# Tail queries and tail x of two batches: transposed by the DMA instead of TensorE

## Chip, cores and metric

The kernel runs on one core of a Trainium2 chip. The metric is the device time in microseconds, the median of several runs. A core has TensorE (PE, matrix multiplication; PEld is its loading of weights), VectorE (DVE), ScalarE (ACT), GpSimd (POOL) and SyncE (SP). SP and POOL issue DMA transfers here; PE writes only to PSUM, so what it transposes has to be copied to SBUF by DVE or ACT.

## The reference

A linear attention with cosine weights, followed by a two-layer network. In short:

```python
batch, n_heads, seq, head_dim = (8, 8, 576, 64)      # q, k, v
phi(x) = concat(relu(x) * cos_w, relu(x) * sin_w)    # 64 -> 128 features
kv  = einsum('bhsf,bhsd->bhfd', phi(k), v);  z = sum over s of phi(k)
num = einsum('bhsf,bhfd->bhsd', phi(q), kv)
den = einsum('bhsf,bhf->bhs', phi(q), z) + 1e-06
x   = (num / den), as [4608 tokens, 512]
out = relu(x @ w_in)**2 @ w_out                      # w_in 512 x 2048, w_out 2048 x 512
```

## The kernel before

A batch has 576 positions. 512 of them are four pieces of 128 (J = 4, pieces j = 0 to 3); the other 64 are the tail (j = 4). The tail's eight heads are laid out as two halves of 64 partitions, so a tail tile has 128 partitions and half the columns. Two batches share one tail tile of the network's input, xTt, so the tails of batches 0 and 1 are multiplied together.

Attention of one piece goes in steps. `att_feat` makes the features of the queries (qp, for the tail qpt): DVE the cosine half (L171), ACT the sine half (L181). The features are then transposed, either by PE (`att_qT_pe`, L284, into the PSUM tile tq) with a copy to qpTp (`att_qT_copy`, L293), or by a DMA on SP's queue (`att_qT`, L267, straight into qpT). `att_d` multiplies them by kvz (num, L310, on PE) and divides (den, rden and x on DVE, L320 to L324; the tail of x is xt). x is transposed in turn, by PE with a copy (`att_x_pe`, L351 and L356, into the PSUM tile tx) or by a DMA on SP's queue (`att_x`, L342), into xT or, for the tail, xTt.

The network runs after it: `gemm1` multiplies xT by the weights w1sb (hps, L383, on PE), ACT applies the relu (rt, L391), DVE squares (gT, L398); `gemm2` and `pair_mm` multiply by w2sb and by sums of its blocks (L432, L456, L525).

The order of work is written out by hand. The network's work is cut into slots, each some 2 us of PE; `gemm1` of batch 0 is slots 0 to 7, `gemm2` of batch 0 is 8 to 15, `gemm1` of batch 1 is 16 to 25 with the tails in the last two, 24 and 25. Pieces of attention of later batches are hung behind a slot with `at(slot, function, ...)`, and `run` issues slot by slot. `plan` does this for all pieces of a batch, from lists of slots: k, f (features of the queries), kv, d (division), and, where the lists t and x are given, the slots of the transposes on PE. Where t and x are empty, the transposes go by DMA. Only batch 1 gives t and x; batch 0's pieces are placed by hand. Each engine takes its own instructions in this order and waits by semaphores for the others; a DMA on SP's queue starts as soon as its sources are written and SP has issued what stands before it.

POOL's queue loads the weights and batches 1 to 3; SP's queue loads batch 0 at the start and batches 4 to 7 later, and carries all DMA transposes.

Of the kernel before, what the change touches and what calls it, by code (L numbers as in the profile page):

```python
# [19 lines left out]
def kernel(  # L20
# [18 lines left out]
    J = S // P  # L39
# [586 lines left out]
    def at(s, fn, *args):  # L626
        after.setdefault(s, []).append((fn, args))
# [9 lines left out]
    def plan(b, k, f, kv, d, t=(), x=(), act_cos=(1, 3), act_v=range(NS)):  # L637


        for j in range(NS):  # L640
            last = j == J or j % 2
            at(k[j], att_k, b, j, feat_cos_act if j in act_cos else feat_cos)
            at(k[j], att_v, b, j, nc.scalar if j in act_v else nc.vector)
            at(f[j], att_feat, b, j)
            if t:
                at(t[j], att_t, b, j)
            elif last:
                at(f[j], att_qT, b, j // 2)
            at(d[j], att_d, b, j)
            if x:  # L650
                at(x[j], att_x_pe, b, j, x[j] > 16)
            elif last:
                at(d[j], att_x, b, j // 2)
        for i in range(2):
            at(kv[i], att_kv, b, i)


    for j in (2, 3):
# [4 lines left out]
    at(2, att_d, 0, 3)  # L663
    at(3, att_x_pe, 0, 3, True, nc.vector.tensor_copy)
    at(12, att_feat, 0, J)
    at(17, att_t, 0, J)
    at(18, att_d, 0, J)
    at(19, att_x_pe, 0, J, True)
    plan(
        1,  # L670
        k=(8, 8, 8, 9, 9),
        f=(4, 5, 6, 12, 13),
        kv=(10, 10),
        d=(11, 13, 15, 17, 19),
        t=(5, 6, 7, 16, 17),
        x=(12, 14, 16, 18, 20),
        act_cos=(),
        act_v=(),
    )
    at(14, load_batch, 3, nc.gpsimd, "qkv")  # L680
    plan(
        2,
        k=(21, 22, 23, 24, 25),
        f=(18, 19, 20, 22, 23),
# [3 lines left out]
        act_v=(1, 3),  # L688
    )
    plan(  # L690
        3,
        k=(29, 31, 32, 34, 35),
        f=(27, 30, 33, 34, 34),
# [4 lines left out]
    for b in range(4, B):  # L698
# [6 lines left out]
            f=(o + 4, o + 4, o + 5, o + 5, o + 6),  # L705
# [99 lines left out]
```

## Time and profile before

| what | before |
|---|---|
| median of 8 runs | 290.05 us (289.21 to 291.23) |
| the profiled execution | 290.23 us, span 288.4 us |
| PE busy | 281.8 us (98%), 3045 matmuls |
| DVE, ACT busy | 202.3 us (70%), 163.6 us (57%) |
| PE's granted clock | 1.00 throughout |
| DMA | 53.04 MB, mean 184 GB/s |

The page is read from the profiled execution. Busy times of an engine are sums of its instructions without overlap; a row of the timeline gives the start in us from the span's start, the duration, the engine, the line, the operation with the tile written and the tile read, and the count where equal instructions are merged. PE's matmuls are pipelined, so a row's duration reaches into the next row.

### The profile page before, as it was taken

What the parts mean: (1) busy time and instruction counts of PE and PEld (TensorE: products, weight loads), DVE (VectorE), ACT (ScalarE), POOL (GpSimd) and SP (SyncE); (2) the same over time, 40 slices, a digit from 0 to 9 for tenths busy, and PEclk for the clock granted to TensorE, in tenths of its full rate; (3) what the DMA queues carried; (4) which work ended last, traced back from release to release, by engine and by line L of the source; (5) the groups of instructions that cost most, each with busy time, mean ns of one, the idle gap of its engine ahead of it and who ended that gap; (6) DMA issues with size and microseconds to landing.
All of it is one profiled execution on the core that took longest, in us unless ns stands there. A gap on an engine that the chain in (4) does not pass through costs nothing.

```text
span 288.4 us, 7293 instructions
## 1 busy us (share of the span) xinstructions
PE 281.8 (98%) x3045; PEld 235.5 (82%) x3045; DVE 202.3 (70%) x452; ACT 163.6 (57%) x249; POOL 38.9 (14%) x67
## 2 busy tenths in 40 slices
PE   8999999999999999999999999999999999999995
PEld 3569845789678888898988888888998988889884
DVE  1367674687499399887597776977677877547485
ACT  3476753579759759455782358835695551155210
POOL 1462503860000000100002000000000000000002
PEclk9999999999999999999999999999999999999999
DMA  7999995999737998899519995399828540300015
GB/s 215 287 205 282 350 209 188 319 370 315 130 107 190 161 327 187 197 287 239 167 76 204 331 189 164 93 251 300 175 70 209 140 49 2 125 23 0 2 73 148
DMA packets 76785, 53.04 MB, mean 184 GB/s; under 512 B 52016, under 2 KB 71984, under 8 KB 76752
## 3 DMA queue, kind: packets, MB, share of 16 engines
q1 hardware_dynamic: 66960, 29.24, 44.4%
q0 software_dynamic: 9648, 23.20, 27.2%
q8 instruction: 24, 0.39, 0.5%
q10 hardware_dynamic: 144, 0.13, 0.1%
q14 instruction: 9, 0.07, 0.1%
HBM read 36.70 MB, written 9.44 MB: 160 GB/s over the span
## 4 chain that ended last, share of the span: by engine, by line
PE 80%; DMA 8%; issue 2%; ACT 2%; POOL 2%; DVE 2%; SPq 2%; ACTq 0%; POOLq 0%
PE hps L383 38%; PE ya L525 9%; PE yc L525 9%; PE yu L525 7%; PE yv L525 5%; PE num L310 3%; DMA q<-in_q_dram 3%; DMA qt<-in_q_dram 3%; PE kz L241 3%; DMA out_dram<-ysb 3%; PE yps L456 2%; SPq L69 1%; PE tq L284 1%; DVE ysb L537 1%; PE yps L432 1%
## 5 line engine op out<-in xcount | busy, mean ns | idle before, releaser
L383 PEld LDWEIGHTS <-w1sb 128*128 128x128 bf16 x1312 | 112.6, 98 | 13.0 <-issue 2.0
L383 PE MATMUL hps<-xT,w1sb 128*128 128x256 bf16 (+1 forms) x1056 | 119.1, 269 | 0.7 <-ACT rt L391 0.2
L391 ACT ACTIVATE rt<-hps 128x1024 bf16<-128x1024 f32 x72 | 73.6, 1022 | 66.1 <-PE hps L383 43.7
L398 DVE TENSOR_TENSOR gT<-rt 128x1024 bf16<-128x1024 bf16 x64 | 44.0, 687 | 21.1 <-ACT rt L391 21.0
L525 PEld LDWEIGHTS <-gs 128*128 128x128 bf16 x480 | 46.7, 98 | 5.6
L525 PEld LDWEIGHTS <-gT 128*128 128x128 bf16 x312 | 29.7, 98 | 3.5
L410 POOL DMA_DIRECT2D out_dram<-ysb x14 | 7.6, 544 | 171.0 <-DVE ysb L537 145.0
L181 ACT ACTIVATE kp<-k,sin_col 128x512 bf16<-128x512 f32 x32 | 22.4, 717 | 3.3 <-DMA k<-in_k_dram 3.3
L324 DVE TENSOR_TENSOR x<-num,rden 128x512 bf16<-128x512 f32 x32 | 22.1, 692 | 1.1
L181 ACT ACTIVATE qp<-q,sin_col 128x512 bf16<-128x512 f32 x32 | 22.1, 721 | 0.7 <-DMA q<-in_q_dram 0.7
L320 DVE TENSOR_SCALAR den<-num 128x8 f32<-128x8 f32 (+1 forms) x40 | 6.5, 164 | 20.8 <-PE num L310 20.6
L521 DVE TENSOR_TENSOR gs<-gT 128x1024 bf16<-128x1024 bf16 x26 | 17.8, 684 | 0.0
L171 DVE TENSOR_SCALAR qp<-q,cos_col 128x512 bf16<-128x512 f32 x32 | 15.2, 501 | 1.7 <-DMA q<-in_q_dram 1.7
L525 PE MATMUL ya<-w2t,gs 128*128 128x256 bf16 x120 | 15.6, 273 | 0.0
L525 PE MATMUL yc<-w2sb,gs 128*128 128x256 bf16 x120 | 15.6, 273 | 0.0
L525 PE MATMUL yu<-w2t,gs 128*128 128x256 bf16 x120 | 15.5, 273 | 0.0
L383 PE MATMUL hps<-xTt,w1sb 128*128 128x128 bf16 x256 | 15.1, 219 | 0.2 <-ACT rt L391 0.2
L200 ACT CAST vext<-v 128x512 bf16<-128x512 f32 x23 | 14.1, 614 | 1.7 <-DMA v<-in_v_dram 1.7
L525 PE MATMUL yu<-w2sb,gs 128*128 128x256 bf16 x112 | 14.5, 273 | 0.0
L576 ACT COPY s<-yu 128x256 f32<-128x256 f32 x14 | 5.2, 372 | 15.6 <-PE yu L525 15.6
L525 PE MATMUL yc<-w2sb,gT 128*128 128x256 bf16 x104 | 13.5, 273 | 0.0
L525 PE MATMUL yv<-w2t,gT 128*128 128x256 bf16 x104 | 13.5, 273 | 0.0
(97 smaller groups left out, 334.8 us busy)
## 6 DMA issues: line engine op xcount, KB each, us to landing
out_dram<-ysb POOLq DMA_DIRECT2D x14, 512.0 KB, 3.9
k<-in_k_dram SPq DMA_DIRECT2D x5, 1024.0 KB, 8.3
v<-in_v_dram SPq DMA_DIRECT2D x5, 1024.0 KB, 9.4
q<-in_q_dram SPq DMA_DIRECT2D x5, 1024.0 KB, 5.6
q<-in_q_dram POOLq DMA_DIRECT2D x3, 1024.0 KB, 12.6
k<-in_k_dram POOLq DMA_DIRECT2D x3, 1024.0 KB, 9.1
v<-in_v_dram POOLq DMA_DIRECT2D x3, 1024.0 KB, 8.8
w1sb<-in_moe_w_in_dram POOLq DMA_DIRECT2D x4, 512.0 KB, 9.2
```

Of the source, the lines that this page charges most:

```text
L171: nc.vector.tensor_scalar(out=dst[:, :, 0:D], in0=src, scalar1=0.0, scalar2=cos_col[:, j : j + 1], op0=ALU.max, op1=ALU.mult,)
L181: nc.scalar.activation(out=dst[:, :, D:F], in_=src, func=ACTF.Relu, scale=sin_col[:, j : j + 1])
L200: copy(out=vx[:, j, h0:h1, 0:D], in_=piece("v", b, j)[:, h0:h1, :])
L241: nc.tensor.matmul(out=kz[:, half, hh * E1 : (hh + 1) * E1], lhsT=lhsT, rhs=rhs, start=(j == 0 and hh == 0), stop=(j == J and hh == HH - 1),)
L310: nc.tensor.matmul(out=out, lhsT=lhsT, rhs=kvz[:, half * HH + hh, :], start=True, stop=True)
L324: nc.vector.tensor_tensor(out=x_of(b, j).rearrange("p (b k) (l d) -> p b k l d", b=n, l=2), in0=n4[:, :, :, 0:D].rearrange("p b (k l) d -> ...
L383: nc.tensor.matmul(out=out, lhsT=w1sb[:, kb, hb * P : (hb + 1) * P], rhs=rhs, start=(kb == 0), stop=(kb == KB - 1),)
L391: nc.scalar.activation(out=rt[:, :, :], in_=hps[:, :, :], func=ACTF.Relu)
L398: nc.vector.tensor_tensor(out=dst, in0=rt[:, :, :], in1=rt[:, :, :], op=ALU.mult)
L410: eng.dma_start(out=dst, in_=y.rearrange("p i c -> p (i c)") if n > 1 else y[:, c0:c1])
L521: nc.vector.tensor_tensor(out=t[:, :, :], in0=in0, in1=in1, op=op)
L525: nc.tensor.matmul(out=acc, lhsT=lhs[:, hb, :], rhs=rhs[:, hb, :], start=(hb == 0), stop=(hb == HB2 - 1),)
```

## The change

The tail (j = 4) of batches 0 and 1 leaves PE. Its query features are transposed by `att_qT`, and its x by `att_x`, both DMAs on SP's queue. In `plan` the test for the lists t and x becomes one for each piece, and batch 1's lists lose their last entry. The pieces 0 to 3 of these batches stay on PE, and the other batches have been on the DMA for all pieces.

```diff
@@ plan
-            if t:
+            if j < len(t):
                 at(t[j], att_t, b, j)
             elif last:
-                at(f[j], att_qT, b, j // 2)
+                at(max(f[j], 15), att_qT, b, j // 2)
             at(d[j], att_d, b, j)
-            if x:
+            if j < len(x):
                 at(x[j], att_x_pe, b, j, x[j] > 16)
             elif last:
                 at(d[j], att_x, b, j // 2)
@@ batch 0
     at(12, att_feat, 0, J)
-    at(17, att_t, 0, J)
+    at(15, att_qT, 0, J // 2)
     at(18, att_d, 0, J)
-    at(19, att_x_pe, 0, J, True)
+    at(18, att_x, 0, J // 2)
@@ batch 1
         d=(11, 13, 15, 17, 19),
-        t=(5, 6, 7, 16, 17),
-        x=(12, 14, 16, 18, 20),
+        t=(5, 6, 7, 16),
+        x=(12, 14, 16, 18),
```

In the instruction order PE loses eight transposes of qpt (L284) and four of xt (L351), each a weight load and a matmul. DVE loses two copies of tq, ACT two copies of tx. SP gains four DMA transposes, ahead of the first one of batch 2.

## Prediction

> **What bounds the kernel now.** I read the page first, for the engine that has no slack.
>
> ```profile
> PE 281.8 (98%) x3045; PEld 235.5 (82%) x3045; DVE 202.3 (70%) x452; ACT 163.6 (57%) x249; POOL 38.9 (14%) x67
> ...
> PE 80%; DMA 8%; issue 2%; ACT 2%; POOL 2%; DVE 2%; SPq 2%; ACTq 0%; POOLq 0%
> ```
>
> TensorE (PE) is busy 281.8 of 288.4 us and is 80% of the chain that ended last. A matmul taken off PE is worth its place in PE's row, unless what replaces it arrives later than PE wants it. So I read PE's timeline where the twelve transposes stand (start, duration, line, tile).
>
> ```profile
> 56.07 1.91 PE L383 MATMUL hps<-xT,w1sb 128*128 128x256 bf16 x16
> 57.81 0.39 PE L284 MATMUL tq<-ident,qpt 128*128 128x128 bf16 x4
> 58.04 0.41 PE L310 MATMUL num<-kvz,qpTp 128*128 128x65 bf16 x8
> 58.28 0.39 PE L284 MATMUL tq<-ident,qpt 128*128 128x128 bf16 x4
> 58.51 1.91 PE L383 MATMUL hps<-xT,w1sb 128*128 128x256 bf16 x16
> 60.34 0.32 PE L310 MATMUL num<-kvz,qpTp 128*64 128x65 bf16 x8
> 60.59 0.40 PE L351 MATMUL tx<-ident,x 128*128 128x128 bf16 x4
> 60.83 1.91 PE L383 MATMUL hps<-xT,w1sb 128*128 128x256 bf16 x16
> 62.58 0.28 PE L351 MATMUL tx<-ident,xt 128*128 128x128 bf16 x2
> 62.78 0.32 PE L310 MATMUL num<-kvz,qpTp 128*64 128x65 bf16 x8
> 63.03 1.92 PE L383 MATMUL hps<-xT,w1sb 128*128 128x256 bf16 x16
> 64.79 0.28 PE L351 MATMUL tx<-ident,xt 128*128 128x128 bf16 x2
> 64.90 5.40 PE L383 MATMUL hps<-xT,w1sb 128*128 128x256 bf16 x48
> 70.14 1.95 PE L383 MATMUL hps<-xTt,w1sb 128*128 128x128 bf16 x32
> ```
>
> The rows overlap: a duration holds the pipeline's depth, and the next row starts before it ends. The distance from start to start is what PE pays. The three groups of 16 from 64.90 to 70.14 take 5.24 us, 1.75 each, and no idle time stands in these rows. The last line is the first reader of the tails, xTt. PE's timeline a little further on, and ScalarE's (ACT's), show the one wait nearby:
>
> ```profile
> 72.32 1.95 PE L383 MATMUL hps<-xTt,w1sb 128*128 128x128 bf16 x32 [0.23 <-ACT rt L391]
> ```
>
> ```profile
> 70.64 0.72 ACT L181 ACTIVATE qp<-q,sin_col 128x512 bf16<-128x512 f32 x1
> 71.26 1.01 ACT L391 ACTIVATE rt<-hps 128x1024 bf16<-128x1024 f32 x1
> ```
>
> PE could have started this group at 70.14 + 1.75 = 71.89; it started at 72.32, when ACT's rt of 71.26 had freed the buffer (ends 72.27). The tails' first reader may therefore slip by 0.43 us at no cost.
>
> **What is removed.** On PE, from start to start. Between the L383 groups at 56.07 and 58.51 lie 2.44 us; 1.75 is the group, 0.26 the eight num of the middle (58.04 to 58.28 is 0.24, and a boundary), so the eight tq are worth 0.43. Between 60.83 and 63.03 lie 2.20: less 1.75 and 0.25 for num, two tx are 0.20. Between 63.03 and 64.90 lie 1.87: less 1.75, two tx are 0.12. Sum 0.43 + 0.20 + 0.12 = 0.75 us. The far bound is the sum of the durations, 8 x 0.219 + 4 x 0.220 = 2.6 us, but as merged in the rows above (0.39 twice, 0.28 twice) it is 1.34, and most of that lies under the next row. I take 0.75 and keep 1.3 as the far end.
>
> The two copies of tq on VectorE (DVE L293, 0.42 us each) and the two of tx on ACT (L356, 0.37 each) go too. They free 0.7 us of DVE and 0.5 of ACT, as the next row starts about 0.08 to 0.12 before the end. Neither is on the path here: DVE is busy 70%, and ACT's rt at 66.85 and 68.60 start 0.2 after the last matmul of their groups, so PE sets them before and after. I cost them at nothing; if they were the cover of something, it could be a gain only.
>
> **What is added.** Four DMA transposes on SP's queue: two of the queries' tails (qpT from qpt, 128 KB each), two of the tails of x (xTt from xt, 64 KB). SP has none of them before and waits from 10.6 to 64.4 for its first transposes, so nothing is queued behind the first two. Their sources are written at 47.4 and 51.45 (DVE L171, the cosine halves; ACT's are earlier). They start then, whatever slot the code names. The same transfers of other batches land after 3.8 to 5.1 us, so they are there by 52.5 and 56.6. Their readers, the num at 60.34 and 62.78, move to 59.9 and 62.15. Even at the longest landing of any transpose of the trace, 9.05 us, they come at 56.5 and 60.5. Cost nothing; without that cover PE would stand still by the difference, since num is in PE's order.
>
> The tails of x are closer. DVE writes them here:
>
> ```profile
> 61.11 0.42 DVE L324 TENSOR_TENSOR xt<-num,rden 128x256 bf16<-128x256 f32 x1
> ...
> 63.55 0.42 DVE L324 TENSOR_TENSOR xt<-num,rden 128x256 bf16<-128x256 f32 x1
> ```
>
> With num earlier by 0.43 and 0.63 they end near 61.1 and 63.4. The reader on PE moves from 70.14 to 69.39 and may slip to 69.82. For the transfer the rows of batches 2 to 7 say:
>
> ```profile
> L342 SPq DMA_TRANSPOSE xTt<-xt x6: 1168/1198/1793, 91.5 to 232.3; - x6
> ...
> DMA to landing us min/median/max: 2.3/2.6/3.0
> ```
>
> That gives 66.0, rising to 66.4: 3.4 us to spare. But these six ran on nearly free DMA engines. From 52 to 72 us POOL's loads of batches 2 and 3 keep them full. The nearest row is the query transpose of batch 2, issued at 64.71; this is the DMA view from 65 to 68.6:
>
> ```profile
> q0 software_dynamic: 399, 1.40, 101.2%
> ...
> qpT<-qp SPq DMA_TRANSPOSE x1, 9.1
> ```
>
> In 3.6 us only POOL's queue (q0) moved; the transpose's first packet is at 68.86, 4.15 after the issue, and it landed after 9.05. So the landing of the second xTt lies between 63.4 + 2.3 = 65.7 and 63.4 + 9.05 = 72.45. An xTt has an eighth of that transfer's bytes, so I take its wait and a free one's end: 4.15, and 1.05 from first packet to landing (the xTt of 91.52: 93.52 to 94.57). That is 68.6: in time, by 1.2 us. I take no stall, and keep 72.45.
>
> The Trainium skill bears on this wait. Its page DMA: Bandwidth & Descriptors, section Queues, rings and completion order, says that each DMA engine goes round between the queues that have work, one packet at a time. By it the second xTt would wait for at most one of POOL's 1 MB transfers; k and v of batch 3 landed 3.47 us apart (65.61, 69.08), and the sum would stay without a stall. The row of 64.71 neither proves nor refutes it.
>
> Another page speaks against the change. VectorE: DVE Perf Modes, sections The three transpose paths and Rules for kernel authors, gives 390 ns to TensorE and 1309 ns to the DMA for a 128x128 block, and advises TensorE wherever PSUM will do. By its price PE would win 12 x 390 ns = 4.7 us, as an estimate; PE's rows above show a pace of 0.057 us for a transpose (0.22 to 0.23 for four).
>
> The batch 2 query transposes now stand behind the two xTt on SP. Each xTt holds SP for 1.2 to 1.8 us; the second starts at 63.4, so they start at 64.6 to 65.2, against 64.71. They landed at 73.8 and 77.1, and their readers are at 78.87 and 82.81: covered by 5 us. The added 0.38 MB delays POOL's last loads by about 1 us (the engines move some 0.38 MB in one); those are read after 79.
>
> **Sum.** The profiled execution takes 290.23 us with a span of 288.4, 1.8 around it, and stands 0.18 over the median of 290.05. Less 0.75 the span is 287.7, the execution 289.5, the median 289.3.
>
> **Rivals.**
> (1) The tails of x come late, the side of a slower kernel. PE stands at the first L383 group on xTt, with all that follows in order. The second group started at 72.32, so the gain is gone when the first starts at 70.57, and the kernel is slower by over 0.87 us from 71.44. Served only after POOL's two output writes (the first landed at 70.64), the tail would land near 71.5: 0.93 over, 291.0. At the bound of 72.45 it is 1.9 over, 291.9. For it: the full DMA engines and the row of 64.71. Against it: the small size, and the issue 1.3 us earlier than that row's.
> (2) ACT's two copies were part of the 0.43 us wait at 72.32, and it goes as well: 290.05 - 0.75 - 0.43 = 288.9. Against it: ACT's rt at 66.85 and 68.60 wait for PE, so the whole chain moves together.
> (3) The gain is swallowed later, at a load or a transfer with a time of its own: 290.05. Against it: after 72 us the chain is PE with short DVE and ACT pieces, and no load is in it.
>
> That the transposes do not leave PE is excluded: the instruction order of the changed kernel has twelve matmuls less.
>
> **How the numbers follow.** No stall and 0.75: chance 0.54, range 288.9 to 289.7. Rival 1: 0.30; rival 2: 0.10; rival 3: 0.06. The range of 288.75 to 291.2 takes in rival 2 and most of rival 1. A change within 0.3%, 0.87 us, is about what a measurement of this kernel cannot tell from none; the main case stands just inside it at 0.75. So it gives 0.28 to faster and 0.26 to the same; rival 2 gives 0.10 to faster, rival 3 0.06 to the same, rival 1 0.21 to slower and 0.09 to the same. Faster 0.38, same 0.41, slower 0.21.
>
> **What would show it.** Right: L383 groups 2.0 us apart where they were 2.44 and 2.20; the first L383 group on xTt near 69.4, without a wait on a DMA; the second near 71.57, still behind ACT. Rival 1: a gap ahead of that group whose releaser is the DMA of xTt, and landings of xTt of 6 us and more. Rival 2: no gap ahead of the second group. Rival 3: 0.75 us early at 72, and not at the end. The prediction is wrong if num in this stage waits for qpT, or if the distance between groups does not shrink.

## The result, and the profile after

The changed kernel is slower: 294.22 us (292.55 to 305.47) against 289.96 us for the kernel before on the same chip. The ratio is 1.0137, 95% interval 1.0112 to 1.0163, about 4 us. Here and below medians and ranges take in every run, while a ratio leaves out runs more than 1.5% above the fastest of their kernel, so that a median can lie further off than its ratio. The profiled execution of the changed kernel took 294.22 us, with a span of 291.9 (before 290.23 and 288.4), so the trace has 3.5 us of the loss to explain.

The page of the changed kernel, busy times and the chain that ended last:

```profile
PE 282.0 (97%) x3033; PEld 236.0 (81%) x3033; DVE 201.6 (69%) x450; ACT 163.3 (56%) x247; POOL 38.9 (13%) x67
...
PE 85%; DMA 6%; ACT 3%; DVE 2%; SPq 2%; issue 1%; ACTq 0%
```

PE has twelve matmuls less and is busy no less: 282.0 us against 281.8. Something made the remaining ones longer. PE's timeline where the transposes stood (start, duration, line, tile, count; in brackets the idle time ahead of the row and what ended it):

```profile
57.45 1.91 PE L383 MATMUL hps<-xT,w1sb 128*128 128x256 bf16 x16
59.28 0.32 PE L310 MATMUL num<-kvz,qpT 128*64 128x65 bf16 x8
59.54 0.40 PE L351 MATMUL tx<-ident,x 128*128 128x128 bf16 x4
59.77 1.91 PE L383 MATMUL hps<-xT,w1sb 128*128 128x256 bf16 x16
61.75 0.32 PE L310 MATMUL num<-kvz,qpT 128*64 128x65 bf16 x8
62.00 7.16 PE L383 MATMUL hps<-xT,w1sb 128*128 128x256 bf16 x64
72.16 5.36 PE L383 MATMUL hps<-xTt,w1sb 128*128 128x128 bf16 x64 [3.00 <-ACT qpt L181]
77.36 1.89 PE L456 MATMUL yps<-w2sb,gT 128*128 128x512 bf16 x8
```

Three things are to be seen. First, the removal is there: the four L383 groups from 62.00 run without a transpose between them. Second, PE is through with them at about 62.00 + 4 x 1.745 = 68.98 and starts the first group on xTt at 72.16, 3.18 us later. The profile names ACT's qpt as what ended the wait (it ended at 72.13), but the second xTt landed at 72.03 by the trace, and the group starts 0.13 after that; in run 2, where the DMA is named, the distance is 0.14. Third, the two groups on xTt take 77.36 - 72.16 = 5.20 us, where they took 3.97 before (and that with the wait of 0.23 behind ACT). The granted clock says why (window; length; busy time of PE, PEld, DVE, ACT, POOL; clock; DMA share; GB/s):

```profile
72.00:73.00 1.00, 0.84 (x16) 0.87 (x17) 0.25 (x1) 0.13 (x1) 0.00 (x0) 1.00 1.02 335
73.00:74.00 1.00, 1.00 (x15) 1.00 (x13) 0.00 (x0) 0.00 (x0) 0.00 (x0) 0.61 1.12 331
74.00:75.00 1.00, 1.00 (x12) 1.00 (x11) 0.00 (x0) 0.16 (x1) 0.00 (x0) 0.50 1.02 350
75.00:76.00 1.00, 1.00 (x13) 1.00 (x11) 0.10 (x1) 1.00 (x2) 0.00 (x0) 0.50 1.04 400
76.00:77.00 1.00, 1.00 (x15) 1.00 (x14) 1.00 (x3) 0.99 (x2) 0.00 (x0) 0.69 1.04 370
```

The 0.61 and 0.69 are means over slices that lie partly at full clock: by the trace the clock fell to 0.50 at 73.21, 1.05 us after PE had gone back to work, and rose to 1.00 at 76.63. It stood at half for 3.41 us. The landing times of the tile answer for the wait itself, in the view of tile xTt:

```profile
L342 SPq DMA_TRANSPOSE xTt<-xt x8: 1169/1200/1882, 60.5 to 235.5; - x8
...
DMA to landing us min/median/max: 2.3/3.0/10.4
```

The two new ones were issued at 60.51 and 62.97 and landed at 70.90 and 72.03, after 10.4 and 9.05 us. The trace has the same for the others that POOL's loads ran beside: the second query tail 50.91 to 61.70 (10.8), batch 2's first query transpose 64.25 to 81.17 (16.9, before 9.05). The first query tail, issued at 46.87 as the loads of batch 2 began, landed after 5.5 us.

POOL's loads suffered as well. The DMA view from 52 to 72 us, of the kernel before and then of the changed one:

```profile
DMA packets 2809, 7.03 MB, mean 351 GB/s; under 512 B 1152, under 2 KB 1152, under 8 KB 2807
...
q0 software_dynamic: 1927, 6.78, 91.1%
```

```profile
DMA packets 2538, 5.18 MB, mean 259 GB/s; under 512 B 1343, under 2 KB 1343, under 8 KB 2536
...
q0 software_dynamic: 1385, 4.89, 95.7%
```

POOL's queue (q0) moved 4.89 MB instead of 6.78 and occupied the engines more. From 66 to 70 us the packet records show 13 to 39 of its 4096-byte packets a microsecond, of 0.23 to 0.71 us on average; before it was about 90, of 0.16 to 0.17 us. Batch 3's k and v landed at 70.30 and 75.18 instead of 65.61 and 69.08.

The sum of the span: slot 16 starts 0.61 us earlier (53.04 for 53.65, a scatter that the runs of this study have, 53.0 to 54.5 in all but run 6); to the end of the xT groups another -0.55; the wait +3.18; the two groups on xTt +1.23. That is +3.25, which is where PE stands at 77.36 (before 74.11). At full clock and with no wait behind ACT the two groups take 3.57 (run 7), so the half clock cost 1.63; the comparison hides 0.40 of it, because before the change these groups waited for ACT. The rest, some 0.2, comes later and was not traced.

### The profile page after: what moved, and what is told of

The parts are those of the page before. It is cut to its first block, busy times and chain, and to the rows that moved or that the text cites. A ratio compares the mean times of both kernels' runs of the same rounds, so it can differ in the third digit from the quotient of the medians.

```text
span 291.9 us, 7281 instructions
## 1 busy us (share of the span) xinstructions
PE 282.0 (97%) x3033; PEld 236.0 (81%) x3033; DVE 201.6 (69%) x450; ACT 163.3 (56%) x247; POOL 38.9 (13%) x67
## 4 chain that ended last, share of the span: by engine, by line
PE 85%; DMA 6%; ACT 3%; DVE 2%; SPq 2%; issue 1%; ACTq 0%
PE hps L383 40%; PE ya L525 9%; PE yc L525 9%; PE yu L525 7%; PE yv L525 4%; DMA qpT<-qpt 4%; PE num L310 3%; DMA q<-in_q_dram 3%; PE kz L241 3%; PE yps L456 2%; PE yps L432 2%; PE yh L432 2%; SPq L69 1%; PE tq L284 1%; DVE ysb L537 1%
## 5 line engine op out<-in xcount | busy, mean ns | idle before, releaser
L383 PEld LDWEIGHTS <-w1sb 128*128 128x128 bf16 x1312 | 114.1, 99 | 15.9 <-issue 4.9
L383 PE MATMUL hps<-xT,w1sb 128*128 128x256 bf16 (+1 forms) x1056 | 118.9, 269 | 0.7 <-ACT rt L391 0.2
L181 ACT ACTIVATE kp<-k,sin_col 128x512 bf16<-128x512 f32 x32 | 22.4, 717 | 3.1 <-DMA k<-in_k_dram 3.1
L383 PE MATMUL hps<-xTt,w1sb 128*128 128x128 bf16 x256 | 16.6, 231 | 3.0 <-ACT qpt L181 3.0
L525 PE MATMUL yu<-w2t,gs 128*128 128x256 bf16 x120 | 15.5, 273 | 0.0
L525 PE MATMUL yc<-w2sb,gs 128*128 128x256 bf16 x120 | 15.5, 273 | 0.0
```

Of the source, the lines that this page charges most:

```text
L181: nc.scalar.activation(out=dst[:, :, D:F], in_=src, func=ACTF.Relu, scale=sin_col[:, j : j + 1])
L383: nc.tensor.matmul(out=out, lhsT=w1sb[:, kb, hb * P : (hb + 1) * P], rhs=rhs, start=(kb == 0), stop=(kb == KB - 1),)
L525: nc.tensor.matmul(out=acc, lhsT=lhs[:, hb, :], rhs=rhs[:, hb, :], start=(hb == 0), stop=(hb == HB2 - 1),)
```

## The experiments

The expectations name four theories. **A**: the two query tails hold up POOL's loads, and xTt waits behind those. **B**: an xTt takes some 9 us by itself in this place. **C**: the loss is not PE's wait for xTt, but the loads, or batch 2's query transposes, coming late. **D**, formed after the first four runs: a transpose on SP's queue and loads on POOL's queue that run at the same time hold each other up, and the transpose lands about when the loads do. A ratio is against the kernel before on the same chip; that kernel's median was 290.14, 290.10 and 290.41 us in the three sets (runs 1 to 4, 5 to 8, 9 and 10).

**1. Only the queries' tails by DMA.** From the changed kernel:

```diff
@@ plan
-            if j < len(x):
+            if x:
@@ batch 0
-    at(18, att_x, 0, J // 2)
+    at(19, att_x_pe, 0, J, True)
@@ batch 1
-        x=(12, 14, 16, 18),
+        x=(12, 14, 16, 18, 20),
```

> Only the two query tails go by DMA; the tails of x are transposed by TensorE as before. Theory A (the query transposes meet POOL's loads, both crawl, POOL's loads slip by 4 to 6 us, and the xTt transposes wait behind them): the loads slip here too (v of batch 3 lands near 75 instead of 69), but no DMA stands ahead of the network's tail, so the gain of the eight tq less a short wait of num for the second qpT remains: 289.4 to 289.9. Theory B (each xTt waits for POOL's backlog by itself, the query tails play no part): 289.4 to 289.7, the loads where they were. Theory C (the loss is late loads or late query transposes of batch 2, not the wait of TensorE for xTt): 292 to 294.

Measured: 300.19 us (295.13 to 305.53), ratio 1.0189 (1.0109 to 1.0269). PE's timeline, the execution of 300.77 us (the six took 295.13 to 305.53, so its waits show where time is lost, and their sizes are those of a long execution):

```profile
63.93 0.32 PE L310 MATMUL num<-kvz,qpT 128*64 128x65 bf16 x8 [2.01 <-DMA qpT<-qpt]
...
88.12 0.62 PE L310 MATMUL num<-kvz,qpT 128*128 128x65 bf16 x8 [7.95 <-DMA qpT<-qp]
```

The part that I had costed at nothing is as bad as the whole. The second query tail landed 12.85 us after its issue, and num stood in PE's order waiting for it. Batch 2's first query transpose landed after 22.4 us, at 88.08, when v of batch 3 (75.71) and both output writes (the later at 88.0) were done, and cost 7.95 us. PE's clock fell to 0.50 here too, at 84.29, within the wait. Of the theories only C had named batch 2's queries, and its size was too small.

**2. Only the tails of x by DMA.**

```diff
@@ plan
-            if j < len(t):
+            if t:
@@ batch 0
-    at(15, att_qT, 0, J // 2)
+    at(17, att_t, 0, J)
@@ batch 1
-        t=(5, 6, 7, 16),
+        t=(5, 6, 7, 16, 17),
```

> Only the two tails of x go by DMA; the query tails are transposed by TensorE as before. Theory A: with POOL's loads in their old place the second xTt lands at 68 to 70 and TensorE waits 0.3 us or less: 289.6 to 290.3. Theory B: it lands at 72 as in the changed kernel, TensorE waits about 3 us and its clock falls after it: 293 to 294.5. Theory C: 290.

Measured: 295.49 us (294.57 to 296.54), ratio 1.0162 (1.0118 to 1.0206).

```profile
75.45 5.30 PE L383 MATMUL hps<-xTt,w1sb 128*128 128x128 bf16 x64 [4.75 <-DMA xTt<-xt]
```

Here the releaser is named as it is, the DMA of xTt. The two landed 9.26 and 10.67 us after their issues with no query tail near. That is against A. The second landed after v of batch 3 (72.08), beside POOL's output writes (73.84 and 75.18). The two groups again take long after the wait, 5.35 us to the next row, with the clock at 0.50 for 3.3 of them.

**3. Batch 3 loaded on SP's queue, behind the tails.** From the changed kernel:

```diff
-    at(14, load_batch, 3, nc.gpsimd, "qkv")
+    at(20, load_batch, 3, nc.sync, "qkv")
```

> The changed kernel, with the loads of batch 3 moved from POOL's queue (slot 14) to SP's queue (slot 20), where they stand behind both xTt and the first query transpose of batch 2. Theories A and B: the DMA engines are free of POOL's backlog when xTt is issued, it lands within 5 us, by 68, and TensorE does not wait for it: 289.1 to 289.6. If the query tails alone still clog the loads of batch 2, the second qpT lands near 60 and costs at most 0.3. Theory C: 292 to 294; a late batch 3 would show as waits of DVE or ACT for k after 80 us.

Measured: 291.91 us (289.87 to 294.86), ratio 1.0026 (0.9989 to 1.0063), not told apart from the kernel before. The profiled execution was the longest of these, 294.86 us, so its waits show where time is lost, and its total is no measure.

```profile
63.99 0.32 PE L310 MATMUL num<-kvz,qpT 128*64 128x65 bf16 x8 [1.15 <-DMA qpT<-qpt]
71.24 1.95 PE L383 MATMUL hps<-xTt,w1sb 128*128 128x128 bf16 x32
...
86.34 0.42 PE L310 MATMUL num<-kvz,qpT 128*128 128x65 bf16 x8 [2.26 <-DMA qpT<-qp]
```

With batch 3 gone from POOL's queue the xTt landed at 69.30 and 69.77, and PE's wait for them is gone. The first, issued at 61.67 while loads of batch 2 and two output writes of POOL were under way (to 69.10), took 7.64 us, more than the 5 expected; the second took 4.56, and it alone speaks against B. The second query tail, issued beside the loads of batch 2, still landed at 63.95 after 11.9 us. The 2.26 us is of my own making: batch 2's second query transpose stood behind the whole of batch 3 on SP.

**4. The kernel before, with the four transposes added and never read.**

```diff
+    at(15, spare, 0, "q")
+    at(15, spare, 1, "q")
+    at(18, spare, 0, "x")
+    at(19, spare, 1, "x")
```

`spare` issues one transpose of qpt or xt on SP's queue, of the same size as the change's, into a tile that nothing reads. PE keeps its twelve transposes.

> The kernel before, with the four DMA transposes of the change added on SP's queue at the same places; their results go to tiles that nothing reads, and TensorE still does its own. Theories A and B: POOL's loads slip as in the changed kernel, the transposes land after 9 to 11 us, and nobody waits for them: 289.9 to 290.4. Theory C: 292 to 294, since the loads and the query transposes of batch 2 are as late as in the changed kernel.

Measured: 292.34 us (291.03 to 296.54), ratio 1.007 (1.0034 to 1.0106). PE's timeline, and the DMA view from 52 to 72 us:

```profile
80.36 0.42 PE L310 MATMUL num<-kvz,qpT 128*128 128x65 bf16 x8 [1.80 <-DMA qpT<-qp]
```

```profile
DMA packets 2431, 5.50 MB, mean 275 GB/s; under 512 B 1147, under 2 KB 1147, under 8 KB 2429
```

Transposes that nobody waits for cost 1.8 us of span (290.2 for 288.4), all of it at batch 2's first query transpose, which landed at 80.31 instead of 73.76. They alone bring the DMA from 351 to 275 GB/s, and v of batch 3 from 69.08 to 74.39. The clock stays at 1.00 after this wait, as it does after those of 1.15 and 2.26 us in run 3 and 1.80 in run 6; it fell after or within those of 3.00, 4.75 and 7.95 us. So C is true in part: the change has a cost that is not in its own readers.

**5. Only the tails of x by DMA, and batch 3 on SP's queue, in two parts.** From run 2:

```diff
@@ ahead of batch 2
-    at(14, load_batch, 3, nc.gpsimd, "qkv")
@@ behind batch 2
+    at(20, load_batch, 3, nc.sync, "q")
+    at(23, load_batch, 3, nc.sync, "kv")
```

> Only the tails of x by DMA (as in the run of x alone), and batch 3 loaded on SP's queue: q at slot 20, k and v at slot 23, behind all three query transposes of batch 2. Theory D (a DMA transpose on SP's queue and a load on POOL's queue that run at once hold each other up, so a transpose lands when the loads of POOL are done, 9 us and more after its issue): no POOL load is left when xTt is issued, it lands within 5 us, TensorE waits for no DMA, and the 0.32 us of four tx are gained: 289.4 to 290.0. Theory B (an xTt takes 9 us whatever runs beside it): 293 to 295.

Measured: 290.36 us (289.65 to 291.15), ratio 1.0000 (0.9982 to 1.0018).

```profile
70.78 1.95 PE L383 MATMUL hps<-xTt,w1sb 128*128 128x128 bf16 x32
72.96 1.95 PE L383 MATMUL hps<-xTt,w1sb 128*128 128x128 bf16 x32 [0.23 <-ACT rt L391]
```

The same two transposes, issued at the same slots as in run 2, landed after 3.5 and 2.35 us instead of 9.26 and 10.67, and the kernel is 5 us faster than run 2. What differs is that batch 3 no longer comes through POOL's queue beside them; its loads now stand behind them on SP. This is the cleanest pair for D, though it does not say whether the queue of the loads matters or only that they run at that time. The 0.32 us that the two removed pairs of tx are worth is below what the times can show.

**6. Batches 2 and 3 on SP's queue.** The changed kernel, with the lines of run 5 and

```diff
-        load_batch(2, nc.gpsimd, "qkv")
+        load_batch(2, nc.sync, "qkv")
```

> The changed kernel with batches 2 and 3 both loaded on SP's queue, where loads and transposes run one behind the other: batch 2 ahead of the first tail query, batch 3 as in the run beside this one. Theory D: every tail transpose lands within about 5 us of its turn, TensorE waits for none of them, and the whole 0.75 us is gained: 289.0 to 289.7. If loads on SP's queue hold transposes up as POOL's do (theory B, or a plain limit of the DMA engines), the second tail query lands after 62 and TensorE waits 2 us or more: 292 to 295.

Measured: 298.64 us (295.09 to 300.55), ratio 1.0238 (1.0187 to 1.0289).

```profile
63.83 0.32 PE L310 MATMUL num<-kvz,qpT 128*64 128x65 bf16 x8 [1.80 <-DMA qpT<-qpt]
```

A miss. The xTt landed in 3.6 and 2.3 us, but the first query tail now stood behind batch 2's loads in SP's own queue, started at 56.88, and landed at 63.79, after 6.9 us, beside the last of these loads (to 60.82) and POOL's output writes of 56.6 to 64; the run does not tell the two apart. Slot 16 also began 2 us late, at 55.71, for a reason that has nothing to do with the tails: PE waited 2.00 us at 42.87 for a load of w2sb. The profile is of the fastest of the six executions, 295.09 us; what the others lost beyond it is not shown. This place for the loads is no remedy; what stands ahead of the transpose has to be short.

**7. Matmuls that nobody needs, in PE's wait.** From the changed kernel:

```diff
+    at(23, fill, 14)
```

Fourteen matmuls on a tile of zeros ahead of the tail groups; their result is not used.

> The changed kernel with 14 matmuls of zeros (512 columns, about 3.0 us, to a PSUM tile that nothing reads) on TensorE just ahead of the network's tail, in the place of its wait for xTt. If the 1.2 us that the two groups on xTt took longer come from the clock that fell after the wait, the granted clock stays at 1.00, the groups take 1.75 us each again, and the time is 1.0 to 1.4 us below the changed kernel's. If they come from the busy DMA engines or ACT, the time stays within 0.3 us of the changed kernel's and the groups stay long.

Measured: 294.46 us (293.0 to 294.69), ratio 1.0126 (1.009 to 1.0162). PE's timeline and the granted clock of the execution of 293.0 us:

```profile
69.59 3.19 PE L214 MATMUL wm<-zeros,ident 128*128 128x512 bf16 x14
72.61 3.74 PE L383 MATMUL hps<-xTt,w1sb 128*128 128x128 bf16 x64
```

```profile
74.00:75.00 1.00, 1.00 (x22) 1.00 (x19) 0.00 (x0) 0.40 (x1) 0.00 (x0) 1.00 0.60 221
75.00:76.00 1.00, 1.00 (x22) 1.00 (x19) 0.35 (x1) 1.00 (x2) 0.00 (x0) 1.00 1.03 399
```

With PE kept at work the clock stays at 1.00, and the two groups take 3.57 us (to 76.18) instead of 5.20. So the half clock followed from the wait. Over all executions it fits: the mean clock of the execution is 0.998 or more in all four here, and 0.991 to 0.994 in seven of ten of the changed kernel (in three of them it is 0.998 to 1.000, so the clock does not fall every time). In the times the gain is not seen: the profiled execution is 1.2 us below that of the changed kernel, the medians are not, and the filler itself ran 0.7 us past the landing of xTt (71.89). The 1.0 to 1.4 us expected from it are not confirmed.

**8. Plain copies in place of run 4's transposes.** Same sizes, same places, from SBUF to SBUF, never read. In `spare`:

```diff
-        nc.sync.dma_start_transpose(out=t[:, :, :], in_=src)
+        nc.sync.dma_start(out=t[:, :, :].rearrange("p k c -> p (k c)"), in_=src)
```

> The run with four unread transposes on SP's queue again, but the two of xt are plain copies of the same 64 KB and the two of the query tails plain copies of 128 KB, at the same places, read by nothing. Theory D with the transpose as the cause: the copies land within 6 us, POOL's loads are done by 70 as before the change, and the query transposes of batch 2 land where they did (73.8): 289.8 to 290.4. If any transfer on a second queue does it: the copies land after 9 us and more, POOL's loads slip to 74 and later, and the query transposes of batch 2 to 80: 291.5 to 293.

Measured: 290.86 us (290.17 to 299.55), ratio 1.0014 (0.9993 to 1.0036). The DMA view from 52 to 72 us:

```profile
DMA packets 2850, 6.89 MB, mean 345 GB/s; under 512 B 888, under 2 KB 1272, under 8 KB 2848
```

The copies landed after 2.0, 7.4, 6.3 and 6.6 us, the transposes of run 4 after 3.5, 9.9, 9.1 and 11.3. So more than half of a tail's long landing is what a plain copy of its size has too beside POOL's loads; the transpose adds 1.5 to 4.7 us. v of batch 3 came at 70.41, 1.3 us later than before, against 5.3 later in run 4. The throughput in this window stays at 345 GB/s; only the transposes take a fifth of it away (run 4).

The time lies between the two expected ranges, and the expectation was missed in two places. Three copies took more than 6 us, and batch 2's first query transpose, expected where it was (73.8), landed at 78.06, 13.7 us after its issue:

```profile
qpT<-qp SPq DMA_TRANSPOSE x1, 13.7
```

It ran beside POOL's second output write, which landed at 77.45 (before 72.00), and from 72 to 77 us the DMA moved 109 GB/s. Its reader on PE stood at 78.56 and just did not wait. So the plain copies pushed POOL's last transfers into a transpose that the kernel before has as well, and the two slowed each other as in run 4; the copies' harm to batch 2 is 4.3 us of landing against 6.6 there, and only the margin hid it.

**9 and 10. All four tails by DMA, with POOL's queue empty when they are needed.** Run 9 is the changed kernel, run 10 the kernel before, both with the lines of run 5 and

```diff
-        load_batch(2, nc.gpsimd, "qkv")
+        load_batch(2, nc.gpsimd, "kvq")
```

Batch 2's k and v now go out from 35.7 us instead of 49.2, as their buffers come free earlier than q's.

> The changed kernel with all four tail transposes kept; batch 2's loads go out earlier, on POOL's queue, in the order k, v, q in the prologue, and batch 3's loads go out on SP's queue behind the x tails (q at slot 20, k and v at slot 23), so that POOL's queue should be empty when a tail transpose is needed. Theory D (a transpose and POOL's loads hold each other up): no wait of PE for a query or x tail, the x tails land within 5 us of their issue, and the gain of the removed TensorE transposes shows: 289.0 to 289.7 us, a ratio of 0.996 to 0.999. Theory B (each x transpose takes 9 us wherever it stands): x tails land at 70 to 72, PE waits 3 us, 292.5 to 294. If POOL's loads are not done early enough, the second query tail lands after 62 and the kernel loses 1 to 2 us: 290.5 to 292.

> The kernel before with the same moves of batch 2's and batch 3's loads and no tail transposes on the DMA. It separates what the moved loads do by themselves: 290.0 to 290.5 us (a ratio of 1.000 to 1.002) if they are hidden. The run with all four tails on the DMA should then be 0.4 to 0.9 us faster than this one under theory D, and 2 us or more slower under theory B.

Measured: run 9 289.80 us (289.29 to 291.0), ratio 0.9978 (0.9960 to 0.9996); run 10 289.93 us (289.36 to 290.43), ratio 0.9984 (0.9970 to 0.9999). Run 9's timeline, then the first xTt group of run 10:

```profile
59.83 0.32 PE L310 MATMUL num<-kvz,qpT 128*64 128x65 bf16 x8
...
62.16 0.32 PE L310 MATMUL num<-kvz,qpT 128*64 128x65 bf16 x8
62.41 7.16 PE L383 MATMUL hps<-xT,w1sb 128*128 128x256 bf16 x64
69.40 1.95 PE L383 MATMUL hps<-xTt,w1sb 128*128 128x128 bf16 x32
71.59 1.95 PE L383 MATMUL hps<-xTt,w1sb 128*128 128x128 bf16 x32 [0.23 <-ACT rt L391]
```

```profile
69.95 1.95 PE L383 MATMUL hps<-xTt,w1sb 128*128 128x128 bf16 x32
```

No wait for a tail is left. The x tails landed in 3.7 and 2.3 us. The query tails still show D: issued at 47.41 and 51.31 beside batch 2's last loads, they landed at 58.37 and 58.96, when those loads did (57.49 to 58.50), and 1.5 us before num wanted the first (59.83). From slot 16's first group (53.58; run 10 53.46) to the first xTt group PE needs 15.82 us, and 16.49 in run 10: the removal gains 0.67. At the last matmul group 0.54 is left:

```profile
283.28 1.04 PE L525 MATMUL ya<-w2sb,gs 128*128 128x256 bf16 x8
```

```profile
283.82 1.04 PE L525 MATMUL ya<-w2sb,gs 128*128 128x256 bf16 x8
```

Yet both spans are 288.2. The last output write was issued 0.55 us earlier in run 9 but landed only 0.27 earlier (286.92 for 287.19), and the rest went after it. In the medians 0.13 us remains, far inside the intervals. Run 9 is the fastest kernel of the study and just faster than the kernel before, but run 10, which keeps PE's transposes, is so too. That the transposes' removal gains anything in the time is not shown; with no tail late, the profiles show what rival 3 had described, a gain on PE that is gone at the end.

## Why the prediction was wrong, by its own steps

**What was removed: right on PE.** The sum of 0.75 us was the right size. Run 9 against run 10 shows 0.67 on PE. In the changed kernel the same stretch shows 0.55 with a wait of some 0.15 for the second query tail (59.77 to 61.75 is 1.98, where the pair took 1.83 one group earlier). The far end of 1.3 was not reached. No gain beyond PE's was seen from the copies on DVE and ACT, as costed; rival 2 is out, for in run 9 the second group still waits 0.23 behind ACT and starts at 71.59, where the prediction without a stall had 71.57.

**The tails of x, "I take no stall": the step that failed.** The working was 63.4 + 4.15 + 1.05 = 68.6. The 4.15 for the wait to a first packet was not the fault: the first transpose packets after 60.51 are at 64.68, 4.17 us after the first xTt was issued, and the second's own came by 65.67 at the latest (a tile is 256 packets, and the 257th since 60.51 is then), 2.7 us after 62.97. The term that was wrong is the 1.05 from first packet to landing, taken from the xTt of 91.5, which had no load beside it, only an output write. From 64.68 to the landings are 6.2 and 7.35 us, and for the second tile at least 6.36 from its own first packet: beside POOL's loads the packets of the transposes trickle (20 to 36 a microsecond from 66 to 72, after 322 in the microsecond from 65). A price without loads was put on the part of the transfer that lay beside loads. Even a plain copy of this size took 6.6 us in this place (run 8), which from 63.4 would be 70.0, past the 69.82 at which PE's slack ends. The prediction held the true landing inside its bounds (72.03 against 72.45) and gave it to rival 1, with the right wait, a gap ahead of the first xTt group, and a chance of 0.30. Its reason for a late landing, that the tail would be served after POOL's two output writes, did not come: these landed at 77.19 and 78.55, after it.

**Rival 1's price: too small.** It counted lateness only: at the measured start of 72.16 it gives 72.16 - 70.57 = 1.59 over. The trace has 3.5 over. It left out that PE's clock can fall after such a wait, which is the 1.63 us seen in the profiled execution and absent in run 7; the remaining 0.2 or so was not traced.

**The query tails, "Cost nothing": wrong.** The longest landing of the trace before, 9.05, was taken as the worst. The change itself made longer ones: 10.8, and 12.85 in run 1, where num waited 2.01 in the profiled execution. The margin of 5 us for batch 2's query transposes ("covered by 5 us") fell for the same reason: 16.9, 22.4 and 15.5 us to land in the changed kernel and runs 1 and 4. In the changed kernel PE was by then so late that it did not wait for them; in runs 1 and 4 it did, by 7.95 (a long execution) and 1.80.

**POOL's loads, "delays by about 1 us": wrong by five.** Bytes over throughput comes near the 1.3 us of the plain copies of run 8. Transposes of the same bytes gave 5.3 (run 4) and 6.1 (the changed kernel). No row of the trace before had shown a price for this, as there only one transpose met the end of the loads. It should have been bounded from that row: the one transpose of 64.71 had taken 9.05 us, and I read it as the transpose's problem alone.

**What was concluded from the round of the queues: not borne out.** The Trainium skill's page DMA: Bandwidth & Descriptors, section Queues, rings and completion order, has the engines go round between queues packet by packet, and I concluded that an xTt would wait for at most one 1 MB transfer. The trace disagrees with that conclusion: between the issue of the second xTt (62.97) and its landing (72.03) v (just ending) and q of batch 2 and k of batch 3 landed, 63.01, 65.91 and 70.30. The skill's page VectorE: DVE Perf Modes, section Rules for kernel authors, advised TensorE, and that advice was right here. Its prices do not say why: the loss is in what the transposes and the loads do to each other, and with no load of POOL beside it a tail of x landed in 2.3 to 3.7 us.

**What stays open.** Why a transpose and POOL's loads slow each other is not in the records. The runs show that a tail of x is late only with transfers of POOL beside it (run 2 against run 5), that four transposes delay the loads by 5 us and plain copies by 1.3 (runs 4 and 8), and that an output write of POOL can be the partner too (run 8). Not every such meeting is slow: in the kernel before the xTt of 91.52 ran beside an output write (91.05 to 94.23) and landed after 3.05 us. Whether POOL's queue is special in this, or any second queue of loads would do the same, was not tried.

## What to carry to other kernels

Before a step moves to a DMA, look at which transfers of other queues run in its window, and take its price from a transfer that ran among them to its landing; if the trace has only half of such a one, the other half is unknown, not free. Cost the harm to the neighbours as well: an unread copy of the new transfer, put into the old kernel, measures it in one run. And a new wait on PE costs more than its length where the clock falls behind it; here waits up to 2.26 us left it at 1.00.

## What was not expected of the hardware

- Transposes of 0.38 MB in all took the DMA from 351 to 259 GB/s over 20 us, and to 275 where nothing read them (run 4); plain copies of the same bytes left 345 (run 8).
- A 64 KB transpose landed in 2.3 to 3.7 us with no POOL loads about (kernel before, runs 5, 6 and 9), and in 8.3 to 11.3 us beside them (changed kernel, runs 2, 4 and 7); batch 2's first query transpose in 3.7 us (run 9) and up to 22.4 us (run 1, a long execution). A plain copy of 64 KB beside the loads took 6.3 and 6.6 us (run 8).
- A wait of PE of 3.0 us was followed, 1.05 us after its end, by 3.41 us at a granted clock of 0.50; after waits of 1.15 to 2.26 us (runs 3, 4 and 6), and with matmuls in the wait (run 7), the clock stayed at 1.00.
